# Token blocks of 512 instead of 256 at the end of the first feed-forward stage and in most of the second

## The chip, the cores and the metric

One NeuronCore of one Trainium2 chip runs the whole program in a single launch. The metric is device time in microseconds (us) from launch to end; the median of three runs is compared. The kernel is written with explicit instructions for five engines: TensorE (PE: matmuls, and their weight loads, PEld), VectorE (DVE), ScalarE (ACT), GpSimd (POOL) and SyncE (SP, which issues the transfers).

## The reference: what is computed

```python
# q, k, v: 4 batches x 8 heads x 576 positions x 64
out_up    = repeat(softmax_attention(mean4(q), mean4(k), mean4(v)), 4)   # on groups of 4 positions
out_local = attention of each position on those less than 4 away
x = (out_up + out_local), heads side by side        # 2304 tokens x 512
h = x @ w_in;   g = where(h > 0, h, exp(min(h, 0)) - 1);   x = g @ w_out   # ELU; 512 -> 2048 -> 512
h = x @ w2_in;  r = max(h, 0);  g = s * r * r + b;          out = g @ w2_out
```

The kernel holds every factor of the feed-forward matmuls as the sum of a high and a low part and multiplies high by high, low by high and high by low. Each product therefore takes three passes on PE.

## The kernel before

**Tiling.** The 2304 tokens are nine blocks of N = 256, numbered j = 0 to 8. Stage ph = 0 is the ELU layer, ph = 1 the squared one; the hidden 2048 are FC = 16 chunks f of 128. The text names a block (ph, j), and (ph, j, f) one chunk of it. For each chunk, `ffn_h` (matmuls at L879) multiplies the block's input x by the first weight into a PSUM tile `h`: 12 matmuls of 256 columns (4 slices of the 512 features, three passes). ACT and DVE apply the activation and split the result into `gh` and `gl`. `ffn_x` then multiplies these by the second weight and adds up in PSUM tiles `acc`. In stage 0 that is 12 matmuls of 256 columns (L935, tokens are the columns). In stage 1 it is 6 of 512 columns (L938, tokens are the rows, and the 512 columns are the output features). Eight PSUM banks are shared by three pools: `ps_t` (2, attention and transposes), `ps_h` (2) and `ps_a` (4).

**Weights.** Chunk f of a layer has a single SBUF buffer `w{f}`. The second layer's chunk can be written into it only when the first layer's last `ffn_x` with that chunk is done. A chunk is loaded into one of two buffers `raw`, worked on by DVE (L357, L362, L364) and ACT, copied to the high part of `w{f}` by ACT, and subtracted for the low part by POOL or DVE, in two halves (`w<-raw,w`). After that its `raw` is free for the load of chunk f + 2.

**Inputs.** The last tokens of stage 0 come from the attention in pieces of 128. They are loaded into `xr`, transposed on PE (L846), added up by DVE (L857), and split into a high part by ACT and a low part by POOL. Stage 1 reads its input from a DRAM tensor `x2d[j]` that stage 0's block j has stored.

**Order.** Blocks 0 and 1 of stage 0 run side by side, block 1 `LB` chunks later. Blocks 2 to 6 follow one by one, and blocks 7 and 8 side by side again (`LASTP = 2`). Stage 1 takes its nine blocks in turn. `ffn_x` of a chunk is issued three chunks after its `ffn_h` (`LAG`). The order on each engine is not written out: `Plan` gives every operation a cost and a due time (`T0`, `P0`, `P1`, `P2` and the other numbers at the file's head) and takes for each engine the ready operation that is due first. Where it foresees PE idle for more than 0.2 us, it puts in dummy matmuls (`keep_warm`, 128 columns, `wz`, L1139). These are instructions like any others: they run whether or not the wait is there.

Of the kernel before, what the change touches and what calls it, by code (L numbers as in the profile page):

```python
# [6 lines left out]
F32 = mybir.dt.float32  # L7
# [14 lines left out]
DIRECT = 2  # L22
# [32 lines left out]
class Plan:  # L55
# [172 lines left out]
def attn_moe_moe2(ctx, tc, q, k, v, w_in, w_out, w2_in, w2_out, s2, b2, mask, mask_d, out):  # L228
# [637 lines left out]

    def ffn_h(ph, j, f, n=N):
        due = vt(ph, j, f)
        third = ph == 0 and 2 <= j < NSUB - LASTP and 3 <= f < FC - 3 and f % 3 == 0
        ps = Buf(ps_a, "acc", [128, n]) if third else Buf(ps_h, "h", [128, n])  # L870
# [20 lines left out]
        for i, (run, need) in enumerate(runs):  # L891
            op("pe", us * len(run), mm(run, i == 0, i == len(runs) - 1), r=need + [ps], w=[ps], u=[w, x], due=due, ffn=True)
        e = Buf(p2, "r", [128, n])
        gh, gl = Buf(p4, "gh", [128, n], F32R), Buf(p4, "gl", [128, n], F32R)
        due -= 4
        ta, td, tp = 0.11 + n / 1200, 0.065 + n / 960, 0.15 + n / 480
        r1, r2, r3 = (Buf(None, "r", None) for _ in range(3))
        if ph == 0:
# [5 lines left out]
                out=e(), in0=e(), scalar=-1.0, in1=ps(), op0=ALU.add, op1=ALU.max), r=[r2, ps], w=[r3], u=[e], due=due)  # L904
            copy(gh, e, n, r=[r3], w=[gh], u=[e], due=due)
            tt(gl, e, lambda: gh().bitcast(F32), ALU.subtract, n, r=[r3, gh], w=[gl], u=[e], due=due)
        else:
# [4 lines left out]
            op("act", ta + 0.1, lambda: nc.scalar.activation(out=gh(), in_=e(), func=ACTF.Identity, bias=sb2[:, 1:2]),  # L912
               r=[r2], w=[gh], u=[e], due=due)
            op("dve", td + 0.07, lambda: nc.vector.scalar_tensor_tensor(  # L914
                out=gl(), in0=e(), scalar=sb2[:, 1:2], in1=gh().bitcast(F32), op0=ALU.add, op1=ALU.subtract),
               r=[r2, gh], w=[gl], u=[e], due=due, lock=True)
        return gh, gl

    def ffn_x(ph, j, f, g):
        gh, gl = g  # L920
        w = w_b[ph, f]
        due = vt(ph, j, f) + 3 * (P1 if ph == 0 else P2)
        if f == 0:
            acc_b[ph, j] = [Buf(ps_a, "acc", [128, 512]) for _ in range(2)]
        for a in range(2):
            acc = acc_b[ph, j][a]

            def pe(acc=acc, a=a):
                for i, (wpart, g) in enumerate(((0, gh), (1, gh), (0, gl))):
                    wo = w()[:, wpart, 1]  # L930
                    last = f == FC - 1 and i == 2
                    if ph == 0:
                        for c in range(2):
                            cc = 2 * a + c
                            nc.tensor.matmul(acc()[:, c * N:(c + 1) * N], lhsT=wo[:, cc * 128:(cc + 1) * 128], rhs=g(),  # L935
                                             start=(f == 0 and i == 0 and c == 0), stop=last and c == 1)
                    else:
                        nc.tensor.matmul(acc(), lhsT=g()[:, a * 128:(a + 1) * 128], rhs=wo,  # L938
                                         start=(f == 0 and i == 0), stop=last)

            op("pe", 0.712, pe, r=[w.out, gh, gl, acc], w=[acc], u=[w], due=due, ffn=True)
            if f == FC - 1:
                o = Buf(p2, "ev", [128, 512])
                if ph == 0:
                    copy(o, acc, 512, r=[acc], w=[o], due=due - 4)
# [3 lines left out]
                    continue  # L949
                parts = 2 if j == NSUB - 1 else 1  # L950
                n = 512 // parts
                for i in range(parts):
                    half, c = Buf(None, "half", None), slice(i * n, (i + 1) * n)
                    copy(lambda o=o, c=c: o()[:, c], lambda acc=acc, c=c: acc()[:, c], n, ("act", "dve")[i:] if parts > 1 else ("act", "dve"),
                         r=[acc], w=[half], u=[o], due=due - 4)
                    load(Buf(None, "out", None), 262144 // parts, lambda a=a, o=o, c=c: nc.sync.dma_start(
                        out=out[j * N + a * 128:j * N + (a + 1) * 128, c], in_=o()[:, c]), due, r=[half], u=[o])

    def load_x(ph, j):
        due = vt(ph, j, 0)  # L960
        xb = x_buf(ph, j)
        cols = []
        t = j * N
        end = (j + 1) * N if ph else min((j + 1) * N, max(j * N, DIRECT * S))
        n = end - t
        while t < end:
            jj, o = divmod(t, HS if ph == 0 else N)
            m = min(end - t, (HS if ph == 0 else N) - o)
            cols.append((xd[divmod(jj, 2)] if ph == 0 else x2d[jj], o, m))
            t += m  # L970
        for c2 in range(2 if n else 0):
            t = Buf(p2, "xr", [128, 2, N])

            def ld(t=t, c2=c2):
                done = 0
                for src, o, m in cols:
                    nc.sync.dma_start(out=t()[:, :, done:done + m],
                                      in_=src.t[c2 * 256:(c2 + 1) * 256, o:o + m].rearrange("(c p) t -> p c t", p=128))
                    done += m

            load(t, 1024 * n, ld, due - 12, r=[c[0] for c in cols], n=len(cols))
            for c in range(2):
                split(xb, 2 * c2 + c, 0, n, lambda t=t, c=c: t()[:, c, :n], [t], due - XL)
        for o in range(n, N, 128) if ph == 0 else ():
            load_direct(xb, o, [divmod((j * N + o) // 64 + g, NT64) for g in range(2)], due)

# [128 lines left out]
    for n, (ph, j, f) in enumerate(order):  # L1115
# [88 lines left out]
```

## Time and profile before

| what | value |
|---|---|
| median of 3 runs | 979.16 us (978.72 to 982.04) |
| the profiled execution | 976.13 us, span 974.0 us |
| granted TensorE clock | 0.999 of full |
| PE busy, weight load busy | 955.4 us (98%), 892.2 us (92%) |
| DVE, ACT, POOL busy | 612.4, 473.0, 409.2 us |
| dummy matmuls | 560 |

The span runs from the first to the last instruction. The profiled execution lies 3.0 us under the median of the runs. A matmul's busy time includes its passage through the array, which overlaps the next matmul. The pace of a stream is therefore read from the distance between starts, and a duration divided by its count only over a long run.

### The profile page before, as it was taken

The numbers are of one execution on the slowest core, as the hardware profiler recorded it, in microseconds if no ns is written. First come the engines' busy times: TensorE is split into PE (matmuls) and PEld (weight loads), VectorE is DVE, ScalarE is ACT, GpSimd is POOL, SyncE is SP. The second block draws the span as 40 slices with busy tenths as digits, with TensorE's granted clock in tenths as the row PEclk, the third lists the DMA queues.
The fourth block names the chain that finished last, engine by engine and source line by source line (L and its number), as shares of the span: only waits on it lengthen the run. The fifth ranks groups of instructions, "written<-read, shape, count | busy, mean of one in ns | idle before, by whom it ended". The sixth has DMA issues, their size and how long they took to land.

```text
span 974.0 us, 21374 instructions
## 1 busy us (share of the span) xinstructions
PE 955.4 (98%) x8420; PEld 892.2 (92%) x8420; DVE 612.4 (63%) x1058; ACT 473.0 (49%) x1239; POOL 409.2 (42%) x385
## 2 busy tenths in 40 slices
PE   8999999999999999999999999999999999999998
PEld 7888898999999999999999999999999999999997
DVE  5689888897787988887367797333334343333332
ACT  6687666555554455444665565333333333333332
POOL 5565556678776887775564543010101010010000
PEclk9999999999999999999999999999999999999999
DMA  9755656553433542443333451000101010100000
GB/s 198 200 141 175 192 162 155 136 161 83 127 99 99 123 110 64 100 115 109 109 131 130 152 183 57 23 28 17 44 1 45 1 44 1 44 2 22 1 23 22
DMA packets 102468, 88.34 MB, mean 91 GB/s; under 512 B 48864, under 2 KB 91872, under 8 KB 102368
## 3 DMA queue, kind: packets, MB, share of 16 engines
q1 hardware_dynamic: 100576, 86.54, 31.7%
q8 instruction: 66, 1.08, 0.5%
q10 hardware_dynamic: 1792, 0.44, 0.2%
q14 instruction: 34, 0.28, 0.1%
HBM read 73.85 MB, written 13.11 MB: 89 GB/s over the span
## 4 chain that ended last, share of the span: by engine, by line
PE 69%; DVE 11%; POOL 6%; issue 6%; DMA 4%; ACT 3%; SPq 1%; POOLq 0%; DVEq 0%; ACTq 0%
PE h L879 31%; PE acc L938 21%; PE acc L935 12%; POOL gl L311 2%; PE acc L879 2%; DVE raw L362 2%; DMA raw<-in_moe_w_out_dram 2%; DVE raw L364 2%; POOL w L311 1%; POOL wu L311 1%; DVE raw L357 1%; DVE w L311 1%; DVE raw L822 1%; DVE r L903 1%; DMA w<-in_k_dram 1%
## 5 line engine op out<-in xcount | busy, mean ns | idle before, releaser
L879 PE MATMUL h<-x,w 128*128 128x256 f32 x3024 | 407.0, 284 | 4.0 <-DVE r L903 2.9
L879 PEld LDWEIGHTS h<-x,w 128*128 128x128 f32 x3024 | 387.0, 188 | 19.1 <-DVE r L903 5.0
L935 PE MATMUL acc<-gh,w 128*128 128x256 f32 x1152 | 188.8, 285 | 0.0
L938 PE MATMUL acc<-w,gh 128*128 128x512 f32 x576 | 181.4, 396 | 0.0
L935 PEld LDWEIGHTS acc<-gh,w 128*128 128x128 f32 x1152 | 157.3, 189 | 2.6 <-issue 1.9
L311 POOL TENSOR_TENSOR x<-xr,x 128x256 fp32r<-128x256 f32 (+2 forms) x47 | 40.9, 892 | 262.5 <-DVE x L305 254.6
L909 DVE SCALAR_TENSOR_TENSOR r<-r,sb,h 128x256 f32<-128x256 f32 x144 | 68.9, 478 | 129.2 <-ACT r L908 129.2
L311 POOL TENSOR_TENSOR gl<-r,gh 128x256 fp32r<-128x256 f32 x127 | 111.7, 884 | 81.8 <-ACT gh L303 77.0
L914 DVE SCALAR_TENSOR_TENSOR gl<-r,sb,gh 128x256 fp32r<-128x256 f32 x144 | 77.8, 541 | 101.8 <-ACT gh L912 101.8
L912 ACT ACTIVATE gh<-r,sb 128x256 fp32r<-128x256 f32 x144 | 73.2, 508 | 101.3 <-PE acc L938 86.2
L908 ACT ACTIVATE r<-h 128x256 f32<-128x256 f32 x144 | 55.0, 382 | 130.2 <-PE h L879 129.8
L935 PE MATMUL acc<-gl,w 128*128 128x256 f32 x576 | 115.6, 282 | 0.0
L938 PE MATMUL acc<-w,gl 128*128 128x512 f32 x288 | 113.5, 394 | 0.0
L938 PEld LDWEIGHTS acc<-w,gh 128*128 128x128 f32 x576 | 99.3, 188 | 13.7
L311 POOL TENSOR_TENSOR w<-raw,w 128x512 fp32r<-128x512 f32 x48 | 66.5, 1397 | 60.3 <-ACT w L303 55.8
L935 PEld LDWEIGHTS acc<-gl,w 128*128 128x128 f32 x576 | 88.6, 188 | 0.0
L903 DVE SCALAR_TENSOR_TENSOR r<-r,h 128x256 f32<-128x256 f32 x124 | 50.7, 414 | 54.3 <-ACT r L901 49.3
L303 ACT ACTIVATE gh<-r 128x256 fp32r<-128x256 f32 x144 | 58.3, 413 | 50.4 <-DVE r L903 27.6
L899 ACT ACTIVATE r<-h 128x256 f32<-128x256 f32 x124 | 46.8, 378 | 66.3 <-PE h L879 39.0
L938 PEld LDWEIGHTS acc<-w,gl 128*128 128x128 f32 x288 | 54.1, 188 | 13.5 <-DVE gl L914 0.3
L822 DVE TENSOR_REDUCE raw<-wu 128x128 f32<-128x896 f32 x36 | 63.6, 1787 | 2.0 <-POOL wu L311 1.9
L901 ACT ACTIVATE r<-r 128x256 f32<-128x256 f32 x144 | 60.0, 417 | 3.9
(144 smaller groups left out, 1170.4 us busy)
## 6 DMA issues: line engine op xcount, KB each, us to landing
raw<-in_moe_w_in_dram SPq DMA_DIRECT2D x32, 512.0 KB
raw<-in_moe_w_out_dram SPq DMA_DIRECT2D x32, 512.0 KB
raw<-in_k_dram SPq DMA_DIRECT2D x17, 320.0 KB
raw<-in_v_dram SPq DMA_DIRECT2D x17, 320.0 KB
x2d<-ev SPq DMA_DIRECT2D x18, 256.0 KB
xr<-x2d SPq DMA_DIRECT2D x18, 256.0 KB
out_dram<-ev SPq DMA_DIRECT2D x16, 256.0 KB
vg<-in_v_dram SPq DMA_DIRECT2D x12, 288.0 KB
```

The lines of the kernel that those rows point to most:

```text
L303: a = (0.11 + n / 1200, lambda: nc.scalar.activation(out=out(), in_=src(), func=ACTF.Copy, scale=scale))
L311: f = lambda e: lambda: e.tensor_tensor(out=out(), in0=in0(), in1=in1(), op=alu)
L822: op("dve", 0.07 + 14 * D / 546, lambda: nc.vector.tensor_reduce(out=vo()[:, WD + j * D:WD + (j + 2) * D].rearrange("p (j d) -> p j d", j= ...
L879: nc.tensor.matmul(ps(), lhsT=w()[:, wpart, 0, c * 128:(c + 1) * 128], rhs=x()[:, xpart, c, :], start=first and i == 0, stop=last and i == ...
L901: op("act", ta, lambda: nc.scalar.activation(out=e(), in_=e(), func=ACTF.Exp, scale=-1.0), r=[r1], w=[r2], u=[e], due=due)
L903: op("dve", td, lambda: nc.vector.scalar_tensor_tensor(out=e(), in0=e(), scalar=-1.0, in1=ps(), op0=ALU.add, op1=ALU.max), r=[r2, ps], w=[ ...
L908: op("act", ta, lambda: nc.scalar.activation(out=e(), in_=ps(), func=ACTF.Relu), r=[ps], w=[r1], u=[e], due=due)
L909: op("dve", td + 0.07, lambda: nc.vector.scalar_tensor_tensor(out=e(), in0=e(), scalar=sb2[:, 0:1], in1=ps(), op0=ALU.mult, op1=ALU.mult), ...
L912: op("act", ta + 0.1, lambda: nc.scalar.activation(out=gh(), in_=e(), func=ACTF.Identity, bias=sb2[:, 1:2]), r=[r2], w=[gh], u=[e], due=due)
L914: op("dve", td + 0.07, lambda: nc.vector.scalar_tensor_tensor(out=gl(), in0=e(), scalar=sb2[:, 1:2], in1=gh().bitcast(F32), op0=ALU.add, o ...
L935: nc.tensor.matmul(acc()[:, c * N:(c + 1) * N], lhsT=wo[:, cc * 128:(cc + 1) * 128], rhs=g(), start=(f == 0 and i == 0 and c == 0), stop=l ...
L938: nc.tensor.matmul(acc(), lhsT=g()[:, a * 128:(a + 1) * 128], rhs=wo, start=(f == 0 and i == 0), stop=last)
```

## The change

Blocks (0, 7) and (0, 8) become one block of 512 tokens, and so do (1, 1) and (1, 2), (1, 3) and (1, 4), (1, 5) and (1, 6), (1, 7) and (1, 8). Block (1, 0) keeps its 256. In such a wide block the matmuls of `ffn_h` have 512 columns, and so have those of `ffn_x` in stage 0; there are four `acc` tiles, two of them from `ps_t`. The input's high part lies in a buffer of the tag `x`, its low part in `nat` or `raw`. The activation works in `wu`, and its two results in `T`, `vw` and `vg` in turn; the attention used these five buffers before. `x2d` has one tensor of 512 tokens for the wide block. `LB` goes from 5 to 6, and nine of the planner's numbers change.

```diff
-T0, P0, LB, TR, R0, P1, P2 = 39.86, 4.909, 5, 35.22, 2.175, 2.551, 2.783
+T0, P0, LB, TR, R0, P1, P2 = 39.86, 5.222, 6, 34.78, 2.175, 2.551, 2.665
...
-    order += [(0, j, f) for f in range(FC) for j in range(NSUB - LASTP, NSUB)]
-    order += [(1, j, f) for j in range(NSUB) for f in range(FC)]
+    order += [(0, NSUB - 2, f) for f in range(FC)]
+    order += [(1, j, f) for j in (0, *range(1, NSUB, 2)) for f in range(FC)]
+    wide = {(0, NSUB - 2), *((1, j) for j in range(1, NSUB, 2))}
...
+    class X:
...
+            if (ph, j) in wide:
+                lo = (p2, "raw") if ph and j % 4 == 3 else (p1, "nat")
+                self.tiles = [Buf(*t, [128, CC, 2 * N], F32R) for t in ((p2, "x"), lo)]
+                self.at = lambda i: self.tiles[i]()
+            else:
+                x = Buf(p2, "x", [128, 2, CC, N], F32R)
+                self.tiles = [x, x]
+                self.at = lambda i: x()[:, i]
...
     def x_buf(ph, j):
         if (ph, j) not in x_b:
-            x = Buf(*((p1, "nat") if (ph, j) == (1, 0) else (p2, "x")), [128, 2, CC, N], F32R)
-            x.part = [(Buf(None, "xhi", None), Buf(None, "xlo", None)) for _ in range(CC)]
-            x_b[ph, j] = x
+            x_b[ph, j] = X(ph, j)
         return x_b[ph, j]
...
-    def ffn_h(ph, j, f, n=N):
+    def ffn_h(ph, j, f):
         due = vt(ph, j, f)
+        n = 2 * N if (ph, j) in wide else N
...
-                    nc.tensor.matmul(ps(), lhsT=w()[:, wpart, 0, c * 128:(c + 1) * 128], rhs=x()[:, xpart, c, :],
+                    nc.tensor.matmul(ps(), lhsT=w()[:, wpart, 0, c * 128:(c + 1) * 128], rhs=x.at(xpart)[:, c, :],
...
+            e = Buf(p2, "wu", [128, n])
+            both = Buf(p1, ("T", "vw", "vg")[len(wides) % 3], [128, 2, n], F32R)
+            gh, gl = Buf(None, "gh", None), Buf(None, "gl", None)
+            gh.view, gl.view = (lambda: both()[:, 0]), (lambda: both()[:, 1])
...
         if f == 0:
-            acc_b[ph, j] = [Buf(ps_a, "acc", [128, 512]) for _ in range(2)]
-        for a in range(2):
+            acc_b[ph, j] = [Buf(*((ps_a, "acc") if a < 2 else (ps_t, "at")), [128, 512]) for a in range(tiles)]
+        last = f == FC - 1
+        for k, a in enumerate((2, 3, 0, 1) if two and last else range(tiles)):
...
+                    if ph == 0 and two:
+                        nc.tensor.matmul(acc(), lhsT=wo[:, a * 128:(a + 1) * 128], rhs=g(), start=first, stop=end)
+                    elif ph == 0:
...
-        drain(LAG + (ph == 0 and j < 2))
+        drain(2 if (ph, j) in wide else LAG + (ph == 0 and j < 2))
```

The order that comes out differs at two places on PE. Names are as in the profile, `x6` counts equal rows, and the number at `w_` is the buffer of a weight chunk. The first place is the entry into block (0, 7). Before, from the transposes of the last 128 tokens on (L935 with `w_3055`, the last weight chunk, ends block (0, 6); `w_840` and `w_904` are chunks 0 and 1):

```order
L846 MATMUL at<-ident,xr 128x128 x4
L935 MATMUL acc<-gh,w_3055 128x256 x4
L935 MATMUL acc<-gl,w_3055 128x256 x2
L935 MATMUL acc<-gh,w_840 128x256 x4
L935 MATMUL acc<-gl,w_840 128x256 x2
L935 MATMUL acc<-gh,w_840 128x256 x4
L935 MATMUL acc<-gl,w_840 128x256 x2
L879 MATMUL h<-x,w_840 128x256 x8
L879 MATMUL h<-x,w_904 128x256 x12
L879 MATMUL h<-x,w_840 128x256 x4
L1139 LDWEIGHTS wz
L1139 MATMUL at<-wz 128x128
```

Now, after `ffn_x` of block (0, 6) and 14 dummies (chunks 0 and 1 are now `w_839` and `w_903`):

```order
L859 MATMUL at<-ident,xr 128x128 x4
L1179 LDWEIGHTS wz
L1179 MATMUL at<-wz 128x128
...
L895 MATMUL h<-x,w_839 128x512 x8
L895 MATMUL h<-nat,w_839 128x512 x4
L895 MATMUL h<-x,w_903 128x512 x8
L895 MATMUL h<-nat,w_903 128x512 x4
```

Before, `ffn_h` of (0, 7, 0) stands ahead of these rows, and the rows hold `ffn_x` of (0, 7, 0) and `ffn_h` of (0, 8, 0) and (0, 7, 1); 37 dummies follow. Now nothing of the wide block stands ahead of the transposes, 26 dummies stand between them and its first `ffn_h`, and 7 more behind its second.

The second place is chunk 15 of block (1, 0), whose weight is the last to be converted (`w_9231` before, `w_8688` now). Before:

```order
L938 MATMUL acc<-w_9089,gh 128x512 x2
L938 MATMUL acc<-w_9089,gl 128x512
L879 MATMUL h<-nat,w_9231 128x256 x12
L879 MATMUL h<-x,w_7788 128x256 x12
L879 MATMUL h<-x,w_7861 128x256 x12
```

Now (`w_8559` is chunk 13, whose `ffn_x` is the last ahead of the dummies, as it was before):

```order
L968 MATMUL acc<-w_8559,gh 128x512 x2
L968 MATMUL acc<-w_8559,gl 128x512
L1179 LDWEIGHTS wz
L1179 MATMUL at<-wz 128x128
...
L895 MATMUL h<-x,w_8688 128x256 x12
L895 MATMUL h<-x,w_7702 128x512 x8
L895 MATMUL h<-nat,w_7702 128x512 x4
```

Here 43 dummies have come in, and the first chunks of the next block are 512 columns wide. In the earlier part of the program, whose instructions are the same but for their order, the first 398 dummies stand at the same places in both. Those that follow, up to the start of block (0, 2), go from 121 to 102. Over the whole program they go from 560 to 590, and the other matmuls fall by 1152.

## Rows read from the trace of the kernel before

**Rows 1.** Page, part 1: engine, busy us, share of the span, instructions
```profile
PE 955.4 (98%) x8420; PEld 892.2 (92%) x8420; DVE 612.4 (63%) x1058; ACT 473.0 (49%) x1239; POOL 409.2 (42%) x385
```

**Rows 2.** Windows: start:end, length; each engine's busy us (instructions); clock, DMA
```profile
0.00:200.00 200.00, 189.57 (x2747) 174.25 (x2748) 159.79 (x311) 130.87 (x406) 116.54 (x130) 1.00 0.66 170
200.00:458.00 258.00, 256.17 (x2240) 249.24 (x2240) 219.12 (x347) 126.89 (x376) 196.57 (x163) 1.00 0.40 106
...
610.00:970.00 360.00, 359.94 (x2272) 324.98 (x2270) 128.84 (x270) 123.23 (x274) 17.42 (x24) 1.00 0.06 20
```

**Rows 3.** Chain that ended last, three blocks: start, us, what
```profile
474.82 2.89 PE h L879 x24
...
652.01 1.44 PE h L879 x12
653.45 2.80 PE acc L938 x12
656.25 2.87 PE h L879 x24
...
701.68 2.87 PE h L879 x24
```

**Rows 4.** Timeline of PE in block (1, 0): start, us, what
```profile
573.41 1.56 PE L879 MATMUL h<-nat,w 128*128 128x256 f32 x12
574.81 0.63 PE L938 MATMUL acc<-w,gh 128*128 128x512 f32 x2
```

**Rows 5.** Waits of the weight load, 475 to 560 us: total, times, longest
```profile
PEld h L879 <- DVE r L903: 3.3, 7, 1.0
```

**Rows 6.** Timeline where blocks (0, 7) and (0, 8) begin
```profile
458.30 1.70 PE L879 MATMUL h<-x,w 128*128 128x256 f32 x12 [0.44 <-DVE r L903]
...
463.44 0.60 PE L846 MATMUL at<-ident,xr 128*128 128x128 f32 x4
...
465.28 0.62 ACT L303 ACTIVATE x<-xr 128x512 fp32r<-128x512 f32 x1
...
465.98 1.31 POOL L311 TENSOR_TENSOR x<-xr,x 128x512 fp32r<-128x512 f32 x1 [3.27 <-ACT x L303]
...
468.94 2.24 PE L1139 MATMUL at<-wz 128*128 128x128 bf16 x37
470.99 3.12 PE L879 MATMUL h<-x,w 128*128 128x256 f32 x24
```

**Rows 7.** Timeline: the second layer's weights, and block (1, 0) near its end
```profile
478.85 1.14 ACT L303 ACTIVATE w<-raw 128x1024 fp32r<-128x1024 f32 x1
...
480.06 2.59 POOL L311 TENSOR_TENSOR w<-raw,w 128x512 fp32r<-128x512 f32 x2 [0.30 <-ACT w L303]
...
585.89 2.78 POOL L311 TENSOR_TENSOR w<-raw,w 128x512 fp32r<-128x512 f32 x2 [4.98 <-ACT w L303]
593.66 2.79 POOL L311 TENSOR_TENSOR w<-raw,w 128x512 fp32r<-128x512 f32 x2 [4.99 <-ACT w L303]
600.84 2.77 POOL L311 TENSOR_TENSOR w<-raw,w 128x512 fp32r<-128x512 f32 x2 [4.40 <-ACT w L303]
...
602.17 1.57 PE L879 MATMUL h<-nat,w 128*128 128x256 f32 x12
```

**Rows 8.** Groups by line, ACT and DVE: count, busy us, mean ns; idle before
```profile
L908 ACT ACTIVATE r<-h 128x256 f32<-128x256 f32 x144 | 55.0, 382 | 130.2 <-PE h L879 129.8 <-DVE gl L914 0.4
...
L912 ACT ACTIVATE gh<-r,sb 128x256 fp32r<-128x256 f32 x144 | 73.2, 508 | 101.3 <-PE acc L938 86.2 <-DVE r L909 15.1
...
L914 DVE SCALAR_TENSOR_TENSOR gl<-r,sb,gh 128x256 fp32r<-128x256 f32 x144 | 77.8, 541 | 101.8 <-ACT gh L912 101.8
L909 DVE SCALAR_TENSOR_TENSOR r<-r,sb,h 128x256 f32<-128x256 f32 x144 | 68.9, 478 | 129.2 <-ACT r L908 129.2
...
L903 DVE SCALAR_TENSOR_TENSOR r<-r,h 128x256 f32<-128x256 f32 x124 | 50.7, 414 | 54.3 <-ACT r L901 49.3 <-POOL gl L311 3.1 <-ACT ds L807 1.4
```

**Rows 9.** Timeline of PE at the end
```profile
969.55 0.39 PE L938 MATMUL acc<-w,gl 128*128 128x512 f32 x1
```

More of the change, by code (lines that the diff above doesn't have):

```diff
@@ L935, in pe @@
                             nc.tensor.matmul(acc()[:, c * N:(c + 1) * N], lhsT=wo[:, cc * 128:(cc + 1) * 128], rhs=g(),
-                                             start=(f == 0 and i == 0 and c == 0), stop=last and c == 1)
+                                             start=first and c == 0, stop=end and c == 1)
                     else:
[L938 to L945, printed above, removed]
+                        nc.tensor.matmul(acc(), lhsT=g()[:, a * 128:(a + 1) * 128], rhs=wo, start=first, stop=end)
+            op("pe", 0.70 if two or ph else 0.712, pe, r=[w.out, gh, gl, acc], w=[acc], u=[w] + gu, due=due, ffn=True)
+            if not last:
+                continue
+            final = ph == 1 and j == NSUB - 2
+            o = Buf(p2, "xr" if final and k < 2 else "ev", [128, 512])
+            if ph == 0:
+                copy(o, acc, 512, r=[acc], w=[o], due=due - 4)
+                if two:
+                    load(x2d[j], 262144, lambda a=a, o=o: nc.sync.dma_start(out=x2d[j].t[a * 128:(a + 1) * 128, :], in_=o()), due, r=[o])
+                else:
                     load(x2d[j], 262144, lambda a=a, o=o: nc.sync.dma_start(
@@ L948, in ffn_x @@
                         in_=o().rearrange("p (c t) -> p c t", c=2)), due, r=[o])
[L949 to L957, printed above, removed]
+                continue
+            parts = 2 if final and k >= 2 else 1
+            n = 512 // parts
+            for i in range(parts):
+                half, c = Buf(None, "half", None), slice(i * n, (i + 1) * n)
+                copy(lambda o=o, c=c: o()[:, c], lambda acc=acc, c=c: acc()[:, c], n, ("act", "dve")[i:] if parts > 1 else ("act", "dve"),
+                     r=[acc], w=[half], u=[o], due=due - 4)
+                load(Buf(None, "out", None), 262144 // parts, lambda a=a, o=o, c=c: nc.sync.dma_start(
+                    out=out[j * N + a * 128:j * N + (a + 1) * 128, c], in_=o()[:, c]), due, r=[half], u=[o])
     def load_x(ph, j):
@@ L961, in load_x @@
         xb = x_buf(ph, j)
[L962 to L983, printed above, removed]
@@ L984, in load_x, with ld @@
[L984 to L985 removed]
+        t0, t1 = j * N, (j + 1 + ((ph, j) in wide)) * N
+        end = t1 if ph else min(t1, max(t0, DIRECT * S))
+        for at in range(t0, end, N):
+            cols = []
+            t, e = at, min(at + N, end)
+            while t < e:
+                if ph:
+                    jj = min(t // N, NSUB - 2)
+                    src, o, m = x2d[jj], t - jj * N, N
+                else:
+                    jj, o = divmod(t, HS)
+                    src, m = xd[divmod(jj, 2)], min(e - t, HS - o)
+                cols.append((src, o, m))
+                t += m
+            n, o = e - at, at - t0
+            for c2 in range(2):
+                t = Buf(p2, "xr", [128, 2, N])
+                def ld(t=t, c2=c2, cols=cols):
+                    done = 0
+                    for src, o, m in cols:
+                        nc.sync.dma_start(out=t()[:, :, done:done + m],
+                                          in_=src.t[c2 * 256:(c2 + 1) * 256, o:o + m].rearrange("(c p) t -> p c t", p=128))
+                        done += m
+                load(t, 1024 * n, ld, due - 12, r=[c[0] for c in cols], n=len(cols))
+                for c in range(2):
+                    split(xb, 2 * c2 + c, o, n, lambda t=t, c=c, n=n: t()[:, c, :n], [t], due - XL)
@@ L988, in attn_moe_moe2 @@
+        for o in range(max(end, t0) - t0, t1 - t0, 128) if ph == 0 else ():
+            load_direct(xb, o, [divmod((t0 + o) // 64 + g, NT64) for g in range(2)], due)
     units = [Unit(b, hp) for b in range(B) for hp in range(HP)]
```

51 lines of the change are left out of this document (30 added, 21 removed).

## The prediction, made before the changed kernel ran

> **What bounds the kernel now.** I read the page first: PE 98% busy, its weight load 92%, no other engine over 63% [rows 1]. That says where to look, not what a stage is worth, so I took the windows next. In the second stage (610 to 970 us) PE stands still for 0.06 us of 360 while DVE and ACT are busy for about a third of the time [rows 2]; from 200 to 458 us its gaps are 1.8 us, from 0 to 200 us 10.4 us [rows 2]. The reader should see three regimes. In the first 200 us PE waits for the attention; then it is nearly full; in the second stage it is full, and time there is the number of matmuls times their pace and nothing else. The granted clock is 1.00 in each stretch [rows 2], which is the 2.4 GHz level.
>
> The chain of waits gives the pace. Twelve matmuls of 256 columns take 1.44 us, 120.0 ns each; twelve of 512 columns take 2.80 us, 233.3 ns each [rows 3]. A block takes 701.68 - 656.25 = 45.43 us [rows 3], and 192 x 120.0 + 96 x 233.3 ns = 45.4 us: the two paces explain it all. In the first stage 256 columns cost the same, 2.89 us for 24 [rows 3].
>
> **Second stage: fewer, longer matmuls.** 256 columns at the clock are 106.7 ns, 512 are 213.3 ns. So a short matmul carries 13.3 ns above the clock, and a long one 20.0 ns. Two short ones (240.0 ns) become one long one. Four wide blocks replace 4 x 2 x 192 = 1536 short matmuls by 768 long ones; `ffn_x` keeps its 768, which are long already. No row shows `ffn_h` with 512 columns. Its bounds are the clock's 213.3 ns (saving 768 x 26.7 = 20.5 us) and twice the short one (saving nothing). The nearest row is `ffn_x` of the same stage, the same shape and the same stationary 128 x 128, so I take 233.3 ns: 768 x 6.7 ns = **5.1 us** saved. That the buffer matters a little is seen in block (1, 0): from `nat`, twelve short ones take 574.81 - 573.41 = 1.40 us, 116.7 ns each [rows 4]. That block moves to `x`, and 192 x 3.3 ns = 0.6 us is lost; it stands in the count below.
>
> A rule to weigh against this: the Trainium skill, "TensorE: Matmul & The Clock Gate", section "Back-to-back issue gap", gives N / 2.4 + 2.5 ns for a warm stream. By it one pays 109.2 and 215.8 ns, a pair saves only 2.5 ns, and 768 pairs save 1.9 us. The rows lie above it at both sizes, by 10.8 and 17.5 ns, so here the measured paces decide.
>
> **What must stay hidden there.** The activation of 256 tokens costs ACT 382 + 508 ns and DVE 478 + 541 ns [rows 8]. At double length it is at most double: 1.78 us and 2.04 us of the 5.60 us that a wide chunk holds PE (24 x 233.3 ns). In the new order `ffn_x` follows its `ffn_h` by three chunks, over 11 us, and the four operations in series are at most 3.8 us. An `h` tile is wanted back after `ffn_x`, `ffn_h`, `ffn_x`, 8.4 us. The two `acc` tiles in `ps_t` have no second pair, but two `ffn_h` (5.6 us) stand between their last matmul and the next use. I put all this at nothing. Were the cover gone, each of 64 wide chunks would show its own wait. The end keeps its form: four `ffn_x` follow the last `ffn_h`, and the last two tiles are still stored in halves behind the last matmul, which now starts at 969.55 us [rows 9].
>
> **Blocks (0, 7) and (0, 8).** The columns alone save 768 short matmuls for 384 long ones, 384 x 6.7 = 2.6 us. Waits go too. From 475 to 560 us the weight load waited seven times, 3.3 us, for DVE to release an `h` tile [rows 5]; 8.4 us in place of 4.3 us between uses should cover that. But two things stand against these 5.9 us, and I follow PE by the clock.
>
> *The entry is later.* The wide block's first matmul needs the high part of all 512 tokens. The last piece was transposed at 463.44, and its high part was done at 465.28 + 0.62 = 465.9, its low part at 467.3 [rows 6]. Before, block (0, 7) began at 458.30 [rows 6] without it. Now `ffn_h` of (0, 7, 0) begins at about 466.0. By 470.99 [rows 6] the old order had done four groups of twelve short matmuls; the new one gets that far at about 472.
>
> *PE's own work to the end of block (1, 0).* Ahead of chunk 15 of (1, 0) stand 32 groups of twelve long matmuls (89.6 us), 15 short `ffn_h` at 1.44 us (21.6), 14 `ffn_x` of 1.40 us (19.6) and 7 + 43 dummies at 55.4 ns (2.05 us for 37 [rows 6]; 2.8 us in all). From 466.0 that is 599.6 us, the earliest start.
>
> *The weight of chunk 15.* ACT began to write the first weight of layer two at 478.85, when `ffn_x` of (0, 8, 0) was over [rows 7]. Now `ffn_x` of (0, 7, 0) ends at 466.0 + 4 x 2.8 + 0.4 + 2.8 = 480.4 us, so chunk 0 is 1.6 us later. Behind it one `raw` buffer serves every second chunk. From the POOL row of chunk 0 (480.06) to that of chunk 14 (593.66) [rows 7] it turned seven times at 16.2 us; the last turn of the other one, from the end at 585.89 + 2.78 to 600.84 + 2.77, took 14.9 us [rows 7]. Chunk 15's first half was ready at 602.2, and its `ffn_h` began at 602.17 [rows 7]: here PE was just served. With the old turns the half is ready at 603.8; with 14.9 us in all seven it would come 9 us earlier. DVE has less to do between the turns: 32 operations of 414 ns [rows 8] become 16 of double length. I take the middle between PE's 599.6 and the weight's 603.8, **601.7 us, so 0.5 us saved** (2.6 saved to 1.6 lost). Behind chunk 15 both orders owe the same. So the 5.9 us saved in this pair of blocks go mostly into the wait for weights.
>
> **The earlier part.** The matmuls are the same, in a slightly other order; 19 dummies less are **1.1 us**. Whether the attention keeps pace with the new due times no row shows. I allow 3 us to each side, a quarter of the 12.3 us of gaps up to 458 us [rows 2].
>
> **Sum.** 5.1 + 0.5 + 1.1 = 6.7 us: the profiled execution's 976.1 us becomes 969.4. The median of the runs is 979.16, 3.0 us above it, and I make the forecast against that: **972.5 us**, 0.7% less. What a measurement of this kernel can tell from no change is 0.5%, 4.9 us, which puts the border at 974.3.
>
> **Rivals.**
> - *512 columns cost as much as twice 256.* The part above the clock grows with the columns (13.3 to 26.6 ns). For it: 13.3 and 20.0 do grow. Against: 233.3 is measured at this shape. The second stage then saves nothing, the pair of blocks waits for weights anyway, and the sum is 1.6 us: 977.6, no change. The page's rule named above, with 1.9 us in the second stage, would give 975.7, no change either.
> - *They cost less.* PE's weight load is nearly always busy under short matmuls (249.2 of 258 us) and has pauses in the second stage (325.0 of 360) [rows 2]. If the weight load sets the short pace, long ones could come near to the clock's 213.3 ns. Half of that, 223 ns, gives 768 x 16.7 = 12.8 us there: 964.8 in sum. Against: `ffn_x` has the same pauses and does not run faster.
> - *The weights come late: slower.* The second layer's chunk can be written only when the wide `ffn_x` is over, and DVE takes its queue in order, so a conversion can be caught behind a wait of the activation. One conversion of delay is half a turn, 7.8 us, all of it at chunk 15 of (1, 0), where PE has no other work. From 6.7 us on the change gains nothing; it is slower than the border from 11.6 us on. Two conversions (15.6 us) would give 988. For it: PE was just served. Against: DVE has more room than before, and the 43 dummies put 2.4 us ahead of that chunk.
> - *The attention falls behind in the first 200 us.* A loss of 3 us or more there leaves 976 or more: no change.
>
> **Chances.** Forecast (968 to 974.3) 0.56, and its slower edge up to 976 0.08; no saving from columns 0.09; cheaper columns 0.09; late weights 0.08, half of it beyond the border; attention behind 0.10. So faster 0.65, within 0.5% 0.31, slower 0.04. The range 966 to 978 leaves out most of the cheaper columns and of the late weights.
>
> **What will show it.** Right: in the second stage runs of twelve `ffn_h` matmuls of 512 columns in 2.80 us, and a wide block in 89.6 us; no wait of PE for DVE inside wide chunks; chunk 15 of (1, 0) starting 131 to 138 us after (0, 7, 0) behind its dummies; (0, 2) to (0, 6) as long as before. Wrong: another pace at 512 columns, a wait for `w` in block (1, 0) longer than 3 us, or an entry into (0, 7) far from 466 us.

## The result, and the profile after

The changed kernel takes 967.04 us (median of 4 runs, 966.35 to 969.03), the kernel before 980.6 us beside it (4 runs, 978.72 to 983.59). The ratio is 0.987, with an interval of 0.9836 to 0.9904. The profiled execution took 966.35 us, its span is 964.5 us. Against the profiled execution of before (976.13, span 974.0) that is 9.8 us less, against the medians 13.6. Later runs of both put the difference of the medians at 10.4 to 10.6 us: part of the 13.6 is that these four runs of before came out some 3 us above its later medians. The last section says what else moves the time.

The page, part 1, of the changed kernel (as [rows 1]):

```profile
PE 947.5 (98%) x7298; PEld 832.3 (86%) x7298; DVE 574.6 (60%) x907; ACT 442.1 (46%) x1072; POOL 413.1 (43%) x367
```

PE has 1122 instructions less and is busy 7.9 us less. The windows (as [rows 2]; the third is the wide block (0, 7), the last the second stage):

```profile
0.00:200.00 200.00, 190.42 (x2772) 175.30 (x2773) 159.08 (x311) 131.13 (x406) 121.20 (x132) 1.00 0.65 170
200.00:458.00 258.00, 255.88 (x2216) 249.18 (x2213) 218.53 (x350) 129.98 (x379) 199.30 (x162) 1.00 0.41 109
458.00:544.00 86.00, 86.00 (x414) 69.77 (x413) 48.05 (x50) 49.20 (x72) 45.77 (x31) 1.00 0.36 117
544.00:600.00 56.00, 54.83 (x359) 47.88 (x358) 47.35 (x57) 31.98 (x55) 30.14 (x22) 1.00 0.46 151
610.00:960.00 350.00, 350.00 (x1503) 282.12 (x1502) 95.35 (x131) 93.34 (x149) 11.01 (x15) 1.00 0.05 16
```

PE shows no gap in the wide block, 1.2 us of gaps in block (1, 0), and none in the second stage. The matmuls of `ffn_h` are now at L895, those of `ffn_x` at L961 (wide, stage 0), L965 (narrow) and L968 (stage 1), the dummies at L1179. The chain that ended last, in block (1, 5) (as [rows 3]; its 16 `ffn_h` begin at 773.04 and those of the next block at 862.52):

```profile
773.04 2.79 PE h L895 x12
775.83 1.40 PE acc L968 x6
777.23 1.40 PE at L968 x6
778.63 2.79 PE h L895 x12
...
862.52 2.79 PE h L895 x12
```

Twelve long `ffn_h` matmuls take 2.79 us, 232.5 to 233 ns each, and the block takes 862.52 - 773.04 = 89.48 us, where two narrow ones took 2 x 45.43 [rows 3]. The timeline at the entry into the wide block, then at the second layer's weights and chunk 15 of (1, 0), then at the end (as [rows 6, 7, 9]):

```profile
34.60 0.95 PE L895 MATMUL h<-x,w 128*128 128x256 f32 x6
...
202.29 0.72 PE L895 MATMUL h<-x,w 128*128 128x256 f32 x4
...
460.27 0.61 PE L859 MATMUL at<-ident,xr 128*128 128x128 f32 x4
...
461.64 0.63 ACT L303 ACTIVATE x<-xr 128x512 fp32r<-128x512 f32 x1 [1.37 <-DVE xr L870]
...
462.33 2.13 PE L895 MATMUL h<-x,w 128*128 128x512 f32 x8
...
477.60 1.12 ACT L303 ACTIVATE w<-raw 128x1024 fp32r<-128x1024 f32 x1
...
479.04 2.57 POOL L311 TENSOR_TENSOR w<-raw,w 128x512 fp32r<-128x512 f32 x2
...
589.85 2.78 POOL L311 TENSOR_TENSOR w<-raw,w 128x512 fp32r<-128x512 f32 x2 [4.66 <-ACT w L303]
...
595.58 2.58 PE L1179 MATMUL at<-wz 128*128 128x128 bf16 x43
595.80 1.15 ACT L303 ACTIVATE w<-raw 128x1024 fp32r<-128x1024 f32 x1 [2.38 <-DVE raw L365]
...
597.02 2.75 POOL L311 TENSOR_TENSOR w<-raw,w 128x512 fp32r<-128x512 f32 x2 [4.40 <-ACT w L303]
597.97 3.54 PE L895 MATMUL h<-x,w 128*128 128x256 f32 x20
601.35 1.09 PE L895 MATMUL h<-nat,w 128*128 128x512 f32 x4
...
958.86 1.56 PE L968 MATMUL acc<-w,vw 128*128 128x512 f32 x6
```

The first two rows are the starts of blocks (0, 0) and (0, 2). Chunk 15 of (1, 0) starts at 597.97, right behind the 43 dummies; its row holds 12 matmuls of 256 columns and 8 of 512, which need 12 x 120.0 + 8 x 233 ns = 3.30 us. To the next row 3.38 us pass, so less than 0.1 us is waited inside. The last of the six matmuls in the last row starts at 960.02. From these rows and those of before the gain falls into three stretches (here and below, a last digit can differ by rounding):

| stretch | before, us | after, us | gain, us |
|---|---|---|---|
| start to the transposes of the last tokens | 463.44 | 460.27 | 3.17 |
| from there to chunk 15 of (1, 0) | 138.73 | 137.70 | 1.03 |
| from there to the start of the last matmul | 367.38 | 362.05 | 5.33 |
| rest of the span | 4.45 | 4.48 | 0.0 |

The groups of the wide activation in stage 1 (count, busy us, mean ns; as [rows 8]):

```profile
L934 DVE SCALAR_TENSOR_TENSOR wu<-wu,sb,h 128x512 f32<-128x512 f32 x64 | 47.9, 748 | 123.8 <-ACT wu L933 123.8
...
L933 ACT ACTIVATE wu<-h 128x512 f32<-128x512 f32 x64 | 38.3, 598 | 123.9 <-PE h L895 123.5
...
L939 DVE SCALAR_TENSOR_TENSOR vw<-wu,sb,vw 128x512 fp32r<-128x512 f32 x22 | 16.5, 752 | 44.0 <-ACT vw L937 44.0
L937 ACT ACTIVATE vw<-wu,sb 128x512 fp32r<-128x512 f32 x22 | 15.9, 724 | 44.0 <-PE at L968 42.4 <-DVE wu L934 1.6
```

ACT works 1.32 us on a wide chunk and DVE 1.50 us, of the 5.59 us that it holds PE. Both lie under the doubled durations that the prediction allowed for.

### The profile page after: what moved, and what is told of

The parts are those of the page before. It is cut to its first block, busy times and chain, and to the rows that moved or that the text cites. A ratio compares the mean times of both kernels' runs of the same rounds, so it can differ in the third digit from the quotient of the medians.

```text
span 964.5 us, 18468 instructions
## 1 busy us (share of the span) xinstructions
PE 947.5 (98%) x7298; PEld 832.3 (86%) x7298; DVE 574.6 (60%) x907; ACT 442.1 (46%) x1072; POOL 413.1 (43%) x367
## 4 chain that ended last, share of the span: by engine, by line
PE 78%; DVE 11%; ACT 4%; POOL 3%; issue 2%; DMA 1%; POOLq 0%; DVEq 0%; SPq 0%; ACTq 0%
PE h L895 33%; PE acc L965 13%; PE acc L968 11%; PE at L968 9%; PE acc L895 3%; DVE raw L363 2%; DVE raw L365 2%; PE at L1179 1%; ACT w L303 1%; DVE raw L358 1%; PE at L727 1%; PE at L961 1%; PE acc L961 1%; DVE raw L835 1%; PE at L628 1%
## 5 line engine op out<-in xcount | busy, mean ns | idle before, releaser
L895 PE MATMUL h<-x,w 128*128 128x256 f32 (+1 forms) x1936 | 340.2, 321 | 2.3 <-DVE r L934 1.1
L895 PEld LDWEIGHTS h<-x,w 128*128 128x128 f32 x1936 | 283.1, 188 | 36.1 <-issue 1.8
L965 PE MATMUL acc<-gh,w 128*128 128x256 f32 x896 | 147.5, 286 | 0.0
L965 PEld LDWEIGHTS acc<-gh,w 128*128 128x128 f32 x896 | 122.4, 189 | 2.9 <-issue 2.5
L934 DVE SCALAR_TENSOR_TENSOR wu<-wu,sb,h 128x512 f32<-128x512 f32 x64 | 47.9, 748 | 123.8 <-ACT wu L933 123.8
L933 ACT ACTIVATE wu<-h 128x512 f32<-128x512 f32 x64 | 38.3, 598 | 123.9 <-PE h L895 123.5
L965 PE MATMUL acc<-gl,w 128*128 128x256 f32 x448 | 90.0, 282 | 0.0
L965 PEld LDWEIGHTS acc<-gl,w 128*128 128x128 f32 x448 | 68.9, 188 | 0.0
L924 ACT ACTIVATE r<-h 128x256 f32<-128x256 f32 x92 | 34.8, 379 | 55.8 <-PE h L895 27.0
L311 POOL TENSOR_TENSOR wu<-raw 128x896 f32<-128x896 f32 x27 | 57.5, 2141 | 6.3 <-DVE raw L835 5.9
L303 ACT ACTIVATE w<-raw 128x1024 fp32r<-128x1024 f32 x32 | 36.5, 1142 | 41.5 <-DVE raw L365 41.3
L363 DVE SCALAR_TENSOR_TENSOR raw<-raw 128x1024 int32<-128x1024 int32 x32 | 47.1, 1473 | 9.2 <-ACT raw L303 7.9
L895 PE MATMUL h<-nat,w 128*128 128x512 f32 x192 | 52.4, 394 | 0.0
L311 POOL TENSOR_TENSOR raw<-xr,x 128x256 fp32r<-128x256 f32 x15 | 11.5, 794 | 86.3 <-DVE x L305 81.3
L365 DVE SCALAR_TENSOR_TENSOR raw<-raw 128x1024 int32<-128x1024 int32 x32 | 46.1, 1442 | 1.1
```

The source lines that it names most:

```text
L303: a = (0.11 + n / 1200, lambda: nc.scalar.activation(out=out(), in_=src(), func=ACTF.Copy, scale=scale))
L311: f = lambda e: lambda: e.tensor_tensor(out=out(), in0=in0(), in1=in1(), op=alu)
L363: nc.vector.scalar_tensor_tensor(out=low(), in0=high(), scalar=-0x80000000, in1=low(), op0=ALU.bitwise_and, op1=ALU.bitwise_or)
L365: nc.vector.scalar_tensor_tensor(out=low(), in0=high(), scalar=3, in1=low(), op0=ALU.logical_shift_left, op1=ALU.bitwise_or)
L933: op("act", ta, lambda: nc.scalar.activation(out=e(), in_=ps(), func=ACTF.Relu), r=[ps], w=[r1], u=[e], due=due)
```

## The experiments

Every kernel is compared with the kernel before on the same chip. The last column holds the times of the executions whose mean granted clock was 0.999 or more; why it is there is told in the last section.

| kernel | median us (runs) | before | ratio [interval] | us at clock 0.999 or more |
|---|---|---|---|---|
| before | 977.24 (27), 977.81 (11), 977.34 (23) | | | 975.22 to 976.93 (9) |
| changed, again | 967.24 (6) | 977.81 | 0.9881 [0.9846, 0.9916] | 965.65, 966.10 |
| changed, third | 966.94 (6) | 977.34 | 0.9895 [0.9864, 0.9926] | none |
| numbers only | 974.58 (12) | 977.24 | 0.9974 [0.9957, 0.9991] | 973.72, 974.12, 974.76 |
| wide, old numbers | 972.49 (12) | 977.24 | 0.9952 [0.9935, 0.9969] | 970.04, 970.47, 970.71 |
| only (0, 7) wide | 973.26 (10) | 977.24 | 0.9955 [0.9937, 0.9972] | 971.57, 971.57 |
| `LB` and `P0` only | 976.05 (12) | 977.34 | 0.9975 [0.9956, 0.9993] | 974.00 |
| other eight numbers | 977.01 (12) | 977.34 | 0.9989 [0.9972, 1.0006] | 975.18 |
| changed with `LB` 5 | 968.13 (6) | 977.81 | 0.9894 [0.9856, 0.9932] | 965.58 |
| no late dummies | 966.00 (6) | 977.81 | 0.9866 [0.9832, 0.9901] | 964.13 |
| mixed, 4 chunks | 965.40 (6) | 977.24 | 0.9877 [0.9847, 0.9906] | 961.70, 963.20 |
| mixed, 4 chunks, again | 965.86 (6) | 977.34 | 0.9871 [0.9841, 0.9900] | 962.15 |
| mixed, 8 chunks | 966.14 (6) | 977.81 | 0.9879 [0.9835, 0.9924] | 963.06 |

The profiled executions, by stretches (us): A from the first `ffn_h` to that of block (0, 2), B from there to the last transposes, C from there to chunk 15 of (1, 0), D from there to the start of the last matmul. A star marks a stretch in which the clock was at its lower level for more than 1 us. In the mixed orders chunk 15 of (1, 0) comes after chunks of (1, 1), so only C + D can be compared.

| kernel | A | B | C | D | C + D |
|---|---|---|---|---|---|
| before | 169.19 | 259.04 | 138.73 | 367.38 | 506.12 |
| changed | 167.69 | 257.98 | 137.69 | 362.06 | 499.75 |
| changed, again | 167.53 | 257.05 | 137.86 | 362.06 | 499.92 |
| changed, third | 167.59* | 256.22 | 137.84 | 362.06 | 499.90 |
| numbers only | 168.04 | 256.97 | 138.50 | 368.98 | 507.48 |
| wide, old numbers | 171.74* | 259.51 | 138.92 | 362.13 | 501.06 |
| only (0, 7) wide | 166.93 | 256.72 | 138.10 | 368.25 | 506.36 |
| `LB` and `P0` only | 167.32 | 258.43 | 138.83 | 367.38 | 506.21 |
| other eight numbers | 172.35* | 257.41 | 138.44 | 368.98 | 507.41 |
| changed with `LB` 5 | 168.01* | 257.09 | 137.16 | 362.06 | 499.22 |
| no late dummies | 167.97 | 256.06 | 136.25 | 364.51* | 500.75 |
| mixed, 4 chunks | 166.72 | 256.07 | | | 496.48 |
| mixed, 4 chunks, again | 166.36 | 256.52 | | | 498.89* |
| mixed, 8 chunks | 170.81* | 256.43 | | | 499.05* |

**The two halves apart.** Theory: the planner's numbers move the part ahead of the wide blocks, the wide blocks move the rest. Rival: the wide blocks do everything, or the numbers do.

The kernel before with all the numbers of the change (`LB` and nine others, of which the first line is shown):

```diff
-T0, P0, LB, TR, R0, P1, P2 = 39.86, 4.909, 5, 35.22, 2.175, 2.551, 2.783
+T0, P0, LB, TR, R0, P1, P2 = 39.86, 5.222, 6, 34.78, 2.175, 2.551, 2.665
...
```

And the changed kernel with all the numbers of before:

```diff
-T0, P0, LB, TR, R0, P1, P2 = 39.86, 5.222, 6, 34.78, 2.175, 2.551, 2.665
+T0, P0, LB, TR, R0, P1, P2 = 39.86, 4.909, 5, 35.22, 2.175, 2.551, 2.783
...
```

> The kernel before with the planner's numbers (and LB = 6) of the changed one; all blocks keep 256 tokens. Theory: the numbers alone move the earlier part, so block (0, 7) is entered about 3 us sooner than before (transposes of the last 128 tokens near 460 instead of 463.4 us), the weights of layer two start as much sooner, and the whole kernel is about 3 us (0.3%) faster. The second stage keeps 45.4 us a block. Rival: the numbers only suit the wide blocks, and alone they change nothing or lose; then the whole gain of the change comes from the wide blocks.

> The changed kernel with the planner's numbers (and LB = 5) of the one before. Theory: the earlier part is as before (transposes of the last 128 tokens near 463.4 us), chunk 15 of (1, 0) starts at 601 to 603 us, and the second stage behind it saves 5 us, so about 5 us (0.5%) faster than before. Rival: the wide blocks bring all of the gain and the numbers none; then it is as fast as the changed kernel, 1.3% under before.

Each half gains alone: 2.7 us and 4.75 us in the medians. The numbers gain 1.2 us in A and 2.1 us in B and lose 1.4 us in C + D, the wide blocks gain 5.1 us there. The two do not add: with the new numbers the wide blocks gain 507.48 - 499.75 = 7.7 us in C + D, with the old ones 506.12 - 501.06 = 5.1 us. So the new numbers suit the wide order and not the narrow one. In D the wide order takes 362.1 us with either set; it is the narrow one that is 1.6 us longer with the new numbers. The trace shows most of the reason: from chunk 15 on it has 786 matmuls of `ffn_x` in place of 780, so six of them (1.40 us) that stood ahead of chunk 15 now stand behind it, and 13 dummies fill the wait there.

**Only block (0, 7) wide.** Theory: the 2.6 us of columns that this pair of blocks saves go into the wait for weights. Rival: they count in full.

```diff
+    order += [(1, j, f) for j in range(NSUB) for f in range(FC)]
+    wide = {(0, NSUB - 2)}
```

> The changed kernel with only (0, 7) wide; the nine blocks of the second stage have 256 tokens. Theory: as the changed kernel up to chunk 15 of (1, 0), then 45.4 us a block, so about 5 us slower than the changed kernel and 4 us (in the profiles) faster than before. Rival: long matmuls bring little by themselves (twice a short one), and the second stage costs the same as in the changed kernel.

C + D is 506.36 us, against 507.48 with the numbers only and 506.12 before: of the 2.6 us, 1.1 us stays by the first, which has the same numbers, and nothing by the second. So most of it goes into the wait, as the theory has it. The chain shows the narrow pace back in the second stage, and the waits from 541 to 640 us show PE held up by DVE in block (1, 0), as it works on the weights there:

```profile
640.62 1.44 PE h L895 x12
642.06 1.40 PE acc L968 x6
643.46 1.44 PE h L895 x12
```

```profile
PE h L895 <- DVE r L934: 2.2, 4, 1.1
```

The time, 973.26 us, is 1.3 us below the kernel with the numbers only, which their intervals do not tell apart. The changed kernel, 6 us faster, differs from this one in the second stage alone.

**Which numbers.** Theory: `LB` and `P0`, which set how blocks 0 and 1 lie beside each other. Rival: the other eight, most of which set when the attention's steps and the loads are due (`P2` spaces the chunks of the second stage).

The kernel before with the new `LB` and `P0`, the kernel before with the other eight new numbers (the expectations call them seven and leave out `WAIT`), and the changed kernel with the old `LB`:

```diff
-T0, P0, LB, TR, R0, P1, P2 = 39.86, 4.909, 5, 35.22, 2.175, 2.551, 2.783
+T0, P0, LB, TR, R0, P1, P2 = 39.86, 5.222, 6, 35.22, 2.175, 2.551, 2.783
```

```diff
-T0, P0, LB, TR, R0, P1, P2 = 39.86, 4.909, 5, 35.22, 2.175, 2.551, 2.783
+T0, P0, LB, TR, R0, P1, P2 = 39.86, 4.909, 5, 34.78, 2.175, 2.551, 2.665
...
```

```diff
-T0, P0, LB, TR, R0, P1, P2 = 39.86, 5.222, 6, 34.78, 2.175, 2.551, 2.665
+T0, P0, LB, TR, R0, P1, P2 = 39.86, 5.222, 5, 34.78, 2.175, 2.551, 2.665
```

> The kernel before with only LB = 6 and P0 = 5.222: the 11 chunks' due times at the start move, the seven other numbers stay. All nine numbers together gave 2.7 us, and the last transposes came about 3 us earlier. If the interleaving of blocks 0 and 1 is what does it (the stretch from the first ffn_h to block (0, 2) fell by 1.5 to 1.7 us in the changed kernel, all of it ahead of block (0, 2)), this kernel gains 1.5 to 3 us, and that stretch is 167.5 to 168 us against 169.19. If it is the other seven, it gains under 1 us, and the stretch stays at about 169.

> The kernel before with the other numbers of the change, LB and P0 as they were: the complement of the kernel with LB and P0 alone. If LB and P0 do it, this one gains under 1 us and the stretch from the first ffn_h to block (0, 2) stays at about 169 us; if the other seven do it, it gains 2 to 3 us. If each gives part, both kernels gain 1 to 2 us.

> The changed kernel with LB back to 5 and all else as it is. Of the dummies up to block (0, 2) behind the first 398, 135 stand in this one, 102 in the changed one and 121 in the one before. Theory: the 2 to 3 us that the numbers saved in the earlier part are LB's (one more chunk of block 0 ahead of block 1), so (0, 2) is entered 2 to 3 us later and the kernel is as much slower than the changed one. Rival: the due times do it; then LB = 5 costs under 1 us.

The other eight move B: it is 256.1 to 258.0 us in all eleven profiles with the new ones, and 258.4 to 259.5 in the three without them. But the eight alone give most of it back behind chunk 15, where D is 1.6 us longer, 1.4 us of it the six `ffn_x` matmuls named above, and their time is not told from no change.

What `LB` and `P0` do is less sure. Their kernel gains 1.3 us in the medians, a little under the 1.5 to 3 us expected. With the new `P0`, A is 166.4 to 168.0 us in all eight profiles without a star there, but the old one has only one such profile, at 169.19. In that difference is work that only changes sides: the eight matmuls of `at<-d` (0.65 us) stand ahead of the first `ffn_h` of (0, 2) before, at 202.03, and behind it in the changed kernel, at 202.94. `LB` at 5 in the changed kernel leaves A at 168.01 with a piece at the lower clock in it, which points to `P0` and not `LB`; one profile does not show it. Its median is 0.9 us higher than that of the changed kernel beside it, well inside both intervals.

This run also bears on what dummies cost in the early part. Behind the first 398 it has 135 of them up to the start of (0, 2), the changed kernel 102, so 33 x 55.4 ns = 1.8 us more. Yet its last transposes come 168.01 + 257.09 = 425.10 us after its first `ffn_h`, and those of the changed kernel 425.67 and 424.58 us in the two profiles without a star. It is one profile, with a later first `ffn_h` (38.23 us against 34.60 and 34.85), so no proof; but it gives no sign that the 33 dummies cost their 1.8 us. They seem to fill waits.

**What the wait for weights is worth.** The 43 dummies ahead of chunk 15 fill a wait for its weight. Theory: PE has nothing else there, so without the dummies nothing is gained, and with other work in their place the wait goes. Rival: the dummies themselves cost their 2.4 us.

No dummies after 400 us of the planner's time:

```diff
+            if t0 > 400:
+                return
```

The last four chunks of block (1, 0) between the first four of (1, 1) (and, in a second kernel, `MIX = 8`):

```diff
-    order += [(1, j, f) for j in (0, *range(1, NSUB, 2)) for f in range(FC)]
+    MIX = 4
+    order += [(1, 0, f) for f in range(FC - MIX)]
+    order += [x for f in range(MIX) for x in ((1, 1, f), (1, 0, FC - MIX + f))]
+    order += [(1, 1, f) for f in range(MIX, FC)]
+    order += [(1, j, f) for j in range(3, NSUB, 2) for f in range(FC)]
```

> The changed kernel without the 90 dummies of its later part (14, 26 and 7 at the entry of (0, 7), 43 ahead of chunk 15 of (1, 0)), 4.9 us of PE's time. Theory: they only fill waits for the last tokens and the last weight, which end when they end, so the time stays (0 to 0.5 us less) and PE is seen idle at the same places. Rival: they overrun the waits, and up to 3 us come back without them.

> The changed kernel, with the last four chunks of (1, 0) taken in turn with the first four of (1, 1), which need only weights converted long before. Theory: PE waits for the weight of chunk 15 of (1, 0) (43 dummies, 2.4 us, and about 1 us more behind them); with other work at hand it loses nothing there, so 3 us faster than the changed kernel. Rival: the wait is a matter of the order and comes back elsewhere (the input of (1, 1), or PSUM); then it is as fast as the changed kernel.

> As the mixed order of (1, 0) and (1, 1), with the last eight chunks of (1, 0) in turn with the first eight of (1, 1). Theory: four chunks were enough to hide the wait for the last weight, and the smaller waits in the middle of (1, 0) (some 1.7 us, PE waiting for the second halves of weights) go too, so 3 to 5 us faster than the changed kernel. Rival: the two wide-chunk results per turn wait for T, vw and vg, and it is no faster than with four.

Without the dummies PE waits in their place. The timeline at chunk 15 (the number in brackets is the idle time before):

```profile
595.27 0.74 PE L897 MATMUL h<-x,w 128*128 128x256 f32 x4 [1.24 <-ACT w L305]
595.29 2.73 POOL L313 TENSOR_TENSOR w<-raw,w 128x512 fp32r<-128x512 f32 x2 [4.38 <-ACT w L305]
...
596.65 4.62 PE L897 MATMUL h<-x,w 128*128 128x256 f32 x16 [0.64 <-POOL w L313]
```

It waits first for the high half of the weight, from ACT, then for the low half, from POOL, 1.9 us in all. In the changed kernel the dummies hold chunk 15 back to 597.97, 1.0 us after ACT's row has ended (595.80 + 1.15 us). But four matmuls later, at about 598.5, the low half is needed, and the first half of POOL's row ends only at about 597.02 + 2.75 / 2 = 598.4. So the weight ends the wait there, and the dummies cost about 0.1 us. The windows of the kernel without them show the granted clock (third from the end) fall behind the wait, which it does not do there in the changed kernel:

```profile
590.00:596.00 6.00, 4.76 (x27) 3.68 (x25) 4.67 (x5) 2.07 (x4) 1.62 (x2) 1.00 0.00 0
596.00:601.00 5.00, 4.37 (x17) 3.83 (x17) 3.02 (x7) 1.20 (x3) 3.97 (x5) 0.66 0.01 3
```

0.66 over 5 us is 3.4 us at the lower level, 1.2 GHz, half of which, 1.7 us, is lost. D is 2.45 us longer, most of it this loss and the 0.64 us wait for POOL. The kernel's median is 1.2 us lower than that of the changed kernel beside it, inside both intervals: whether these dummies help or cost is not settled.

In the mixed kernel, PE does `ffn_h` of (1, 1) where the dummies were, and no dummies are left there. The rows at 598.04 and 614.92 begin with chunks 13 and 15 of (1, 0); the POOL row is the weight of chunk 15, done 10.8 us before it is used:

```profile
592.44 2.02 PE L899 MATMUL h<-x,w 128*128 128x512 f32 x8
...
598.04 3.47 PE L899 MATMUL h<-x,w 128*128 128x256 f32 x20
...
601.37 2.77 POOL L311 TENSOR_TENSOR w<-raw,w 128x512 fp32r<-128x512 f32 x2 [4.86 <-ACT w L303]
...
614.92 3.47 PE L899 MATMUL h<-x,w 128*128 128x256 f32 x20
```

C + D falls by 3.3 us to 496.48. In the two other profiles of mixed orders it is 498.89 and 499.05, each with one piece of 3.4 us at the lower clock in it, which costs up to 1.7 us. The medians fall less:

> The kernel with the last four chunks of block (1, 0) between the first four of (1, 1), again, beside the changed kernel in the same call. If the wait for weights is worth the 2.4 us of 43 dummies and some 0.9 us of stalls, it is 2 to 3.3 us faster than the changed kernel; if the clock's stretches at half eat it, the two agree within 1 us in the medians.

> The changed kernel again, as the mate of the mixed one: 967 us, ratio to before 0.988.

> The changed kernel itself, timed on the same chip as the others. All theories: about 1.1 to 1.3% under the kernel before; it is the mark for the three other kernels.

Beside the changed kernel on the same chip the mixed one is 1.1 us faster (965.86 and 966.94), between the two cases that were expected. Over all runs the mixed kernel's median is 965.60 us (12 runs) and the changed kernel's 967.04 us (16 runs), 1.4 us apart, and the intervals of their ratios to before overlap. At a full clock they are 961.70 to 963.20 (3) and 965.65 to 966.35 (3): 4 us apart. So the mixed order is the better one where the clock holds, and not told apart by the medians. Eight chunks in place of four bring no more (966.14 us, 963.06 at a full clock), against the 3 to 5 us expected.

## Why the prediction was right, point by point

The forecast was 972.5 us in a range of 966 to 978, and faster; the time is 967.04 us. In profiled executions it was 6.7 us less, and it is 9.8 us.

- **Second stage, 5.1 us: right.** The disputed step was the price of 512 columns in `ffn_h`, taken as 233.3 ns from [rows 3]. It is 232.5 to 233 ns. D fell by 5.33 us, and PE has no gap in D in either kernel, and 780 matmuls of `ffn_x` in both, so only the columns of `ffn_h` are left. The rivals at twice 256 (240 ns) and at 223 ns are both out, and so is the 1.9 us from N / 2.4 + 2.5 ns. The Trainium skill, "TensorE: Matmul & The Clock Gate", section "Back-to-back issue gap", gives that formula for an isolated matmul and says that a stream of weight loads and matmuls, which this kernel is (7298 of each), is spaced otherwise, about 131 ns at 512 columns. The trace agrees with neither: it has 120.0 and 232.5 to 233 ns, where the formula gives 109.2 and 215.8.
- **What must stay hidden there: right.** No wait of PE for the activation shows inside a wide block, and a block takes 89.48 us against the 89.6 foreseen.
- **Blocks (0, 7) and (0, 8), 0.5 us: right, 1.03 us.** The entry was to lag the last transposes by 466.0 - 463.44 = 2.6 us and lags by 2.06. Chunk 15 was to start 131 to 138 us after (0, 7, 0), and starts 597.97 - 462.33 = 135.64 us after it, between PE's own work (133.6) and the old turns of `raw` (137.8). The prediction took the middle of its two bounds, 135.7 us, without a reason for the middle: that this is hit to 0.1 us is luck, that the start lies between them is not. The 0.5 us beyond the forecast is the entry, which came that much sooner behind the transposes. The weight sets it: ACT's first row moved from 15.4 to 17.3 us behind the transposes, and the last POOL row came 117.98 us after the first, not 120.78 [rows 7], 2.8 us gained in the turns. The waits for DVE moved into block (1, 0): from 544 to 602 us the weight load shows

```profile
PEld h L895 <- DVE r L934: 1.7, 3, 0.9
```

  and the timeline has one of these waits behind a step of the conversion (`raw`):

```profile
572.76 1.23 DVE L365 SCALAR_TENSOR_TENSOR raw<-raw 128x1024 int32<-128x1024 int32 x1
...
574.30 0.47 DVE L934 SCALAR_TENSOR_TENSOR r<-r,sb,h 128x256 f32<-128x256 f32 x1
...
574.83 1.49 PEld L895 LDWEIGHTS h<-x,w 128*128 128x128 f32 x12 [0.32 <-DVE r L934]
```

  So DVE has both the weights and the activation to do there; in the wide block (475 to 544 us) there is none of the 3.3 us of [rows 5].
- **The earlier part, 1.1 us: mis-sized, 3.17 us** (4.02 in the second profile of the changed kernel). Both lie inside the 3 us that the prediction allowed to each side, but the runs do not bear out the reason for its 1.1 us, 19 dummies less: with `LB` at 5, 33 dummies more show no cost up to the last transposes. (Of the 121 of before, 20 stand not ahead of (0, 2) but behind its first eight matmuls, at 205.45.) What they do show is the due times, which the prediction left at nothing. The other eight numbers take 1.1 to 2.1 us off B, so (0, 2) to (0, 6) did not stay as long as before; `LB` and `P0` take 1.2 to 1.9 us off A by single profiles, of which 0.65 us only changes sides. 0.6 us lies ahead of the first `ffn_h` (35.20 before, 34.60 now), 0.35 us in the second profile. Where a plan's numbers change, nothing was too low a middle.
- **The base.** The forecast added the 3.0 us by which the runs of before lay above their profile. That was right for the kernel before (9 executions at a full clock from 975.22 to 976.93, medians 977.2 to 980.6) and too much for the changed kernel, whose profile of 966.35 lies 0.7 us under its median. Of the miss of 5.5 us, 3.1 us is the mis-sized gain and 2.3 us the base.
- **Late weights and attention behind: did not come.** DVE had room: it is busy for 48.05 of 86 us in the wide block.

## What to carry to other kernels

Where PE streams without a gap, a stage's time is matmuls times pace: take the pace of the nearest shape from distances of starts in the trace, for 256 and 512 columns apart, and multiply. What a block saves ahead of a wait for something else (here the second layer's weights) can go into that wait, and shows up once the wait is filled with other work, as in the order that mixes two blocks (4 us at a full clock). A planner's numbers are part of the change: test them alone and on top of the edit. Here they gave 2.7 us of some 10.5 alone and about 5 us on top of the wide blocks (972.49 to 967.24 us). And do not count dummies left out as time saved before a run shows it.

## What the runs showed of the hardware

**The granted clock falls to half in some executions and not in others of the same program.** The windows of the mixed kernel's profile:

```profile
0.00:28.00 28.00, 25.47 (x464) 22.24 (x465) 15.47 (x52) 18.78 (x94) 14.77 (x33) 1.00 0.99 219
28.00:44.00 16.00, 14.44 (x185) 13.48 (x183) 10.83 (x14) 6.65 (x13) 8.37 (x7) 0.68 0.52 96
```

And that of the kernel with `LB` and `P0` only:

```profile
24.00:42.00 18.00, 18.00 (x218) 16.64 (x213) 9.92 (x16) 9.47 (x35) 8.68 (x11) 0.53 0.71 164
```

0.68 over 16 us is 10 us at 1.2 GHz, 0.53 over 18 us is 17 us. The first `ffn_h` then starts at 40.87 and 41.55 us, in the profile of the changed kernel at 34.60: some 6 to 7 us later. Before it fell in the mixed kernel, PE had been busy for 25.47 of 28 us, 11.5 us of that with dummies; in the profile of the changed kernel PE is busy for 25.25 us of the same 28, and the clock does not fall there. The third profile of the changed kernel has such pieces ahead of its first `ffn_h` (at 35.94 us) and in A. The first profiles of before and of the changed kernel have no such piece ahead of their last microseconds, so their difference (9.8 us) is cleaner than that of the medians: executions at a clock of 0.999 or more give a middle value of 975.6 for before and 966.1 for the changed kernel, 9.5 us apart. Why it falls in one execution and not in the next stays open.
